# A gated attention kernel: the down-projection computed transposed, its result turned by transposing DMA copies

## Chip, cores, metric

The kernel runs on one core of one Trainium2 chip. The metric is the device time of one execution in microseconds (us), the median of several runs; lower is better.

## What is computed

S = 2048 tokens with D = 640 features, 32 heads of 20, a GLU with F = 1728 hidden features. All inputs and the output are bf16.

```python
xn  = layernorm(x)                         # (2048, 640)
q, k, v = split(xn @ wqkv)                 # 32 heads of 20
s   = softmax(q k^T / sqrt(20)) v  @ wo    # attention, then output projection
h   = sigmoid(xn @ w_gate) * (xn @ w_up)   # (2048, 1728)
g   = silu(h @ w_down)                     # the down-projection, then the gate
out = x + s * g
```

The softmax of 2048 x 2048 scores for 32 heads is most of the work.

## The kernel before

**Stages.** A first stage normalizes x, transposes it into `xnT` (features on partitions, four chunks of QC = 512 tokens) and computes the first keys, values and queries. The main stage works through NBLK = 32 blocks, each a group of GH = 4 heads times a chunk of 512 queries. A block has 64 score jobs (4 heads x 16 key tiles of 128): a matmul of TensorE (L889) into a PSUM bank, an exponential of the 128x512 scores, and a matmul with the values into `oacc` (L926). Most jobs have their exponential on ScalarE (`pt`, two jobs in one instruction, or `px`, one job; L82). The others go to VectorE, which builds the exponential from the bits of an integer: it converts the scores to int16 (`iv`, L1325) and makes three passes over four jobs at a time (`pb`, L1019, L1022, L1025). A short tail at the end does the last block and the last chunk's output.

**Order.** The order of instructions on TensorE, ScalarE, VectorE and GpSimd is written out at build time by a planner: a loop over simulated time in steps of 0.02 us that gives each engine its next instruction by fixed costs (`T_F`, `T_MM`, `T_IV` ...). Beside the score jobs it has a list of items: projections (`mk_k`, `mk_q`, `mk_v` ...), the GLU (`mk_gu`, `mk_down`) and the output (`mk_out`). An item is a chain of steps, such as matmuls on TensorE into one of three flexible PSUM banks, `bk`, then ScalarE, then VectorE; the planner puts it in between where TensorE has room. The same banks take score jobs for VectorE and for `px`. `LEAD` limits by how many us of work the GLU may run ahead of its due time. `M_ORD`, `DORD` and `XORD` choose the order in which banks are tried for an item, a VectorE job and a `px` job. On the chip each engine runs its list strictly in order and waits on semaphores.

**Transfers.** All but two of the main stage's transfers are issued by SP, one queue in order; an SP instruction whose data or buffer is not ready holds up everything behind it. The list `timed` holds transfers that the planner issues at a later simulated time. Per block there are: the softmax sums to DRAM and back (`ld`, L961; `lt`, L963), their reciprocals out and broadcast back (`rt`, L969; `rd`, L971; `rl`, L974), the normalized block into `oU` (L1009), and the next queries (`q`, L644, L645).

**The down-projection.** For each chunk of 512 tokens, after the 14 tiles of the hidden features `hT` are done, `mk_down` makes 8 items (4 token tiles `t4` x 2 halves `h` of the 640 features). Each multiplies a 128-token slice of `hT` (as weights) with 320 columns of `wd` in 14 steps; `cols` issues each step as four matmuls, one for each group of 32 output partitions. Then ScalarE takes a tanh (`td`, 128x320), and VectorE forms (tanh + 1) * ps, four times the silu, with tokens on partitions. For chunks 0 to 2 the product goes in fp32 into one of three buffers `gqs` (L740) and is stored to `gq_dram` (L742); `load_out` brings it back for the output stage (L771), where VectorE multiplies it with the projected attention (`otmp`, L795) and GpSimd adds x (L800). For chunk 3 it stays in SBUF, in two tiles `gql` (L736), and the tail reads it (L1096, L1102). `flush("o")` issues the additions that wait for GpSimd. SBUF tiles with a tag and `bufs=n` rotate through n buffers; a new one waits until the old contents have been read.

Of the kernel before, what the change touches and what calls it, by code (L numbers as in the profile page):

```python
# [27 lines left out]
UH = 6  # L28
UC = UH * DH

URGENT, ROUNDS, HOLD, SLACK, LEAD, LAG, D_LAST, D_LAST_END = 0.2, 6, 0.0, 0.0, 40.0, 2.0, 20, 20
M_ORD, WAIT3, FALL, M_END = 1, 0.2, 1, 2.0
NPT, NPX, NPB, NIV = 12, 5, 3, 3
XMAX, DQ, DORD, XORD, STARVE = 2, 1.4, 2, 0, 0.3

FILL_AT = 40
LOG2E = 1.4426950408889634
# [14 lines left out]
def kernel(  # L52
# [38 lines left out]
    persist = ctx.enter_context(tc.tile_pool(name="persist", bufs=1))  # L91
    wk = ctx.enter_context(tc.tile_pool(name="wk", bufs=2))

    gq_dram = dram.tile([S, D], FP32, name="gq_dram", tag="gqd", bufs=1)
    NU = (HEADS - PG * GH) // UH
    kD = [dram.tile([UC, S], BF16, name=f"kD{u}", tag=f"kD{u}", bufs=1) for u in range(NU)]
    qD = [dram.tile([UC, S], BF16, name=f"qD{u}", tag=f"qD{u}", bufs=1) for u in range(NU)]
# [346 lines left out]
    EL, PL = 0.15, 0.21  # L444
    T_F, T_PV, T_MM, T_MODE = 0.2133, 0.2133, 0.2133, 0.107
    T_IV, T_ON = 0.605, 0.60
    LATE, T_LT, T_OU, T_L2, T_RL = 1.0, 9.0, 1.5, 4.5, 5.6
    T_PASS = (0.1333, 0.1333, 0.27)

    def t_exp(n):  # L450
# [20 lines left out]
    def cols(out, lhsT, rhs, start, stop):  # L471
        for j in range(0, P, 32):
            nc.tensor.matmul(out[j:j + 32, :], lhsT=lhsT[:, j:j + 32], rhs=rhs, start=start, stop=stop,  # L473
                             tile_position=(0, j), skip_group_check=True)
# [189 lines left out]
    def mk_gu(c, kf, at):  # L664
        st = {}
        fs = fsz[kf]
        k2, ko = divmod(kf, 2)

        def alloc0():
            if (c, k2) not in wgu_tiles:  # L670
                load_wgu(c, k2)
            st["g"] = misc_ps()

        def alloc1():
            st["u"] = misc_ps()
            if ko == 0:
                n = c * NK2 + k2 + 1
                if n < NQC * NK2:
                    load_wgu(*divmod(n, NK2))

        def mm(key, i, kd):
            w = wgu_tiles[(c, k2)]
            cols(st[key], w[:, i, kd, ko * P:ko * P + P], xnT[:, c, kd, :], kd == 0, kd == KD - 1)

        def th():
            st["t"] = w2.tile([P, QC], BF16, tag="tnh", bufs=2, name="tnh")
            act_imm(st["t"][0:fs, :], st["g"][0:fs, :], ACT.Tanh, 0.5)

        def ev():
            return nc.vector.scalar_tensor_tensor(out=hT[0:fs, kf, :], in0=st["t"][0:fs, :], scalar=1.0,  # L690
                                                  in1=st["u"][0:fs, :], op0=ALU.add, op1=ALU.mult)

        def mm2(kd):
            cols(st["g"], wgu_tiles[(c, k2)][:, 0, kd, P:2 * P], xnT[:, c, kd, :], kd == 0, kd == KD - 1)

        def th2():
            st["t"] = w2.tile([P, QC], BF16, tag="tnh", bufs=2, name="tnh")
            act_imm(st["t"][fs:P, :], st["g"][0:fs, :], ACT.Tanh, 0.5)

        def ev2():  # L700
            return nc.vector.scalar_tensor_tensor(out=hT[0:fs, kf, :], in0=st["t"][fs:P, :], scalar=1.0,
                                                  in1=st["g"][fs:P, :], op0=ALU.add, op1=ALU.mult)
        if fs < P:
            return [Item([("PE", alloc0, [(T_MM, lambda kd=kd: mm2(kd)) for kd in range(KD)]),
                          ("ACT", 0.48, th2), ("DVE", 0.60, ev2, "free", mark("h", c, kf))], at)]
        return [Item([("PE", alloc0, [(T_MM, lambda kd=kd: mm("g", 0, kd)) for kd in range(KD)]),
                      ("ACT", 0.48, th, "free", mark("t", c, kf))], at),
                Item([("PE", alloc1, [(T_MM, lambda kd=kd: mm("u", 1, kd)) for kd in range(KD)]),
                      ("DVE", 0.60, ev, "free", mark("h", c, kf))], at, gates={1: [("t", c, kf)]})]

    gq_l = []

    def gq_last(t4):
        if len(gq_l) == t4 // 2:
            w = w2.tile([P, 2, KD, 2 * P], BF16, tag="wgu", bufs=2, name="gql")
            gq_l.append(w.rearrange("p i k f -> p (i k f)").bitcast(FP32))
        return gq_l[t4 // 2][:, t4 % 2 * D:(t4 % 2 + 1) * D]

    def mk_down(c, t4, h, at):
        st = {}  # L720
        tt = 4 * c + t4

        def alloc():
            st["ps"] = misc_ps()

        def mm(kf):
            cols(st["ps"][:, 0:HD], hT[:, kf, t4 * P:(t4 + 1) * P], wd[:, kf, h * HD:(h + 1) * HD],
                 kf == 0, kf == NFT - 1)

        def th():  # L730
            st["td"] = w2.tile([P, HD], BF16, tag="td", bufs=2, name="td")
            act_imm(st["td"], st["ps"][:, 0:HD], ACT.Tanh, 0.25)

        def ev():
            if c == NQC - 1:
                return nc.vector.scalar_tensor_tensor(out=gq_last(t4)[:, h * HD:(h + 1) * HD], in0=st["td"], scalar=1.0,  # L736
                                                      in1=st["ps"][:, 0:HD], op0=ALU.add, op1=ALU.mult)
            flush("o")
            gqs = w2.tile([P, HD], FP32, tag="gqs", bufs=3, name="gqs")
            ins = nc.vector.scalar_tensor_tensor(out=gqs, in0=st["td"], scalar=1.0, in1=st["ps"][:, 0:HD],  # L740
                                                 op0=ALU.add, op1=ALU.mult)
            nc.sync.dma_start(out=gq_dram[tt * P:(tt + 1) * P, h * HD:(h + 1) * HD], in_=gqs)  # L742
            return ins
        return Item([("PE", alloc, [(0.14, lambda kf=kf: mm(kf)) for kf in range(NFT)]),
                     ("ACT", 0.32, th), ("DVE", 0.40, ev, "free", mark("d", c, t4, h))], at, pre=[("h", c, kf) for kf in range(NFT)])


    FL, FG, FK = (NG - 1) * GC, (NG - 2) * GC, (KD - 1) * P
# [15 lines left out]
    def load_out(tt):  # L764
        if tt in out_tiles:
            return
        o2 = xfl[:, tt % 3 * KD * QC:tt % 3 * KD * QC + 3 * D]
        flush("o")
        out_tiles[tt] = (o2[:, 0:D], o2[:, D:3 * D].bitcast(FP32))
        nc.sync.dma_start(out=out_tiles[tt][0], in_=x2[tt * P:(tt + 1) * P, :])  # L770
        nc.sync.dma_start(out=out_tiles[tt][1], in_=gq_dram[tt * P:(tt + 1) * P, :])  # L771

    def mk_out(tt, h, at):
# [13 lines left out]
        def ev():  # L787
            xr, gqr = out_tiles[tt]
            sl = slice(h * HD, (h + 1) * HD)
            while sum(x[1] == "o" for x in pool_q) > 2:  # L790
                x = next(x for x in pool_q if x[1] == "o")
                pool_q.remove(x)
                x[2]()
            tmp = w2.tile([P, HD], FP32, tag="gqs", bufs=3, name="otmp")
            ins = nc.vector.scalar_tensor_tensor(out=tmp, in0=st["ps"][:, 0:HD], scalar=0.25,  # L795
                                                 in1=gqr[:, sl], op0=ALU.mult, op1=ALU.mult)

            def part(i):
                cs = slice(h * HD + i * HD // 2, h * HD + (i + 1) * HD // 2)
                add = nc.gpsimd.tensor_tensor(out=xr[:, cs], in0=tmp[:, i * HD // 2:(i + 1) * HD // 2], in1=xr[:, cs], op=ALU.add)  # L800
                if h == 1 and i == 1:
                    nc.sync.dma_start(out=out2[tt * P:(tt + 1) * P, :], in_=xr)
                return add
            for i in range(2):
                pool_q.append((now + 0.6, "o", lambda i=i: part(i)))
            return ins
        return Item([("PE", alloc, [(0.136, lambda kd=kd: mm(kd)) for kd in range(KD)]),
                     ("DVE", 0.40, ev, "free", mark("o", tt, h))], at, need=ALT + 1 + 2 * (tt // 4),
                    pre=[("d", tt // 4, t4, i) for t4 in range(4) for i in range(2)] + [("h", 2, kf) for kf in range(NFT)] + (
                        [("o", tt - 2, 1)] if h == 0 and tt > 1 else []))  # L810


# [1 line left out]
    for c in range(NQC):  # L814
        for kf in range(NFT):
            glu.append(lambda at, c=c, kf=kf: mk_gu(c, kf, at))
        for h in range(2):
            for t4 in range(4):
                glu.append(lambda at, c=c, t4=t4, h=h: [mk_down(c, t4, h, at)])
    for t in range(4 * NVP):  # L820
        v_at[(0, t)] = 0.0
    items = [mk_v(0, list(range(t, min(t + 3, TT))), 0.0) for t in range(4 * NVP, TT, 3)]
# [270 lines left out]
    xg = xl.rearrange("p (t u) -> p t u", u=D)  # L1093

    def t_main(t4):
        nc.vector.scalar_tensor_tensor(out=tmps[t4], in0=mains[t4], scalar=0.25, in1=gq_last(t4)[:, 0:512],  # L1096
                                       op0=ALU.mult, op1=ALU.mult)
        if t4 < 2:
            nc.gpsimd.tensor_tensor(out=tail[t4][:, 0:512], in0=tmps[t4], in1=tail[t4][:, 0:512], op=ALU.add)

    def t_rest(i):
        nc.vector.scalar_tensor_tensor(out=tmp[:, 2 * i:2 * i + 2, :],  # L1102
                                       in0=rest[i][:, 0:2 * EX].rearrange("p (t e) -> p t e", e=EX),
                                       scalar=0.25, in1=gq_l[i].rearrange("p (t u) -> p t u", u=D)[:, :, 512:D],
                                       op0=ALU.mult, op1=ALU.mult)
        (nc.vector if i else nc.gpsimd).tensor_tensor(out=xg[:, 2 * i:2 * i + 2, 512:D], in0=tmp[:, 2 * i:2 * i + 2, :],
                                                      in1=xg[:, 2 * i:2 * i + 2, 512:D], op=ALU.add)
# [420 lines left out]
```

## Time and profile before

| | |
|---|---|
| time, median of 3 runs | 803.18 us (802.27 to 803.32) |
| the profiled execution: its time, and its span from first to last instruction | 803.98 us, 802.3 us |
| granted TensorE clock | 1.000 |
| stores `gq_dram<-gqs` | 24 of 160 KB |
| loads `xnT<-gq_dram` | 12 of 320 KB |
| down-projection matmuls `bk<-wd,hT` | 1792, 128x320 |
| `td` on ScalarE, `gqs` and `gql` on VectorE | 32; 24 and 8, 128x320 |
| DMA queue q1, packets, data, share of 16 engines | 91447, 58.52 MB, 26.1% |

How to read the profile: PE is TensorE (PEld its weight loads), DVE VectorE, ACT ScalarE, POOL GpSimd, SP SyncE, whose DMA instructions stand as SPq. Rows of groups show line, engine, operation, output and inputs by the program's names with shape and type, a count, then busy time in us and mean duration of one in ns, then the idle time ahead of them and what ended it. Rows of the timeline start with the start time and the duration in us. Instructions of one engine overlap, so a duration is longer than the distance to the next start.

### The profile page before, as it was taken

To read this page: it belongs to the slowest core of one execution; us is meant where nothing else is said; L and a number is where in the kernel's file an instruction comes from. 1 tells how busy PE (TensorE), PEld (TensorE's weight loads), DVE (VectorE), ACT (ScalarE), POOL (GpSimd) and SP (SyncE) were. 2 spreads that over 40 slices of the span, in tenths; PEclk is the share of its full clock that TensorE was granted. 3 is DMA by queue.
4 is the path that set the end of the run, shared out by engine and by line. 5 is a ranking of instruction groups with operands and counts; after the bars stand their busy time and mean duration, and the time that the engine had idled before them with its cause. 6 is when DMAs were issued, how large, how long until landed. Compare 5 with 4: busy or idle time off the path is not lost.

```text
span 802.3 us, 25398 instructions
## 1 busy us (share of the span) xinstructions
PE 780.6 (97%) x10466; PEld 285.1 (36%) x10466; DVE 769.5 (96%) x1239; ACT 781.6 (97%) x991; POOL 106.2 (13%) x219
## 2 busy tenths in 40 slices
PE   8899999999999999999999999999999999999997
PEld 5523333333433323334332332333333233333333
DVE  7799999999999999989999999999999999999996
ACT  8799999999999999999999999999999999999994
POOL 7200000000000000000000010000000100502325
PEclk9999999999999999999999999999999999999999
DMA  5441212223122223222113133222311332330421
GB/s 162 133 130 49 69 40 75 63 66 81 47 63 66 73 72 100 52 57 71 49 47 94 53 86 76 76 79 58 98 37 61 91 89 53 106 103 23 141 62 62
DMA packets 91851, 60.47 MB, mean 75 GB/s; under 512 B 34891, under 2 KB 85627, under 8 KB 91735
## 3 DMA queue, kind: packets, MB, share of 16 engines
q1 hardware_dynamic: 91447, 58.52, 26.1%
q8 instruction: 82, 1.34, 0.7%
q14 instruction: 34, 0.28, 0.1%
q10 hardware_dynamic: 288, 0.33, 0.1%
HBM read 45.18 MB, written 11.09 MB: 70 GB/s over the span
## 4 chain that ended last, share of the span: by engine, by line
PE 48%; ACT 39%; DVE 6%; issue 5%; DMA 1%; SPq 0%; POOL 0%; DVEq 0%; ACTq 0%; POOLq 0%
ACT pt L82 31%; PE bk L473 20%; PE scA L889 15%; PE oacc L926 10%; ACT px L82 4%; ACT tnh L82 2%; DVE iv L1325 2%; DVE pb L1025 1%; PE bk L889 1%; ACT td L82 1%; PE tp L292 1%; DVE pb L1022 0%; DMA xt<-in_A_x_dram 0%; PE scrap L398 0%; PE psk L142 0%
## 5 line engine op out<-in xcount | busy, mean ns | idle before, releaser
L82 ACT ACTIVATE pt<-scA 128x1024 bf16<-128x1024 f32 (+1 forms) x709 | 708.8, 1189 | 1.0 <-PE scA L889 0.4
L1325 DVE TENSOR_SCALAR iv<-bk 128x512 int16<-128x512 f32 x500 | 332.9, 684 | 12.0 <-PE bk L889 9.6
L889 PE MATMUL scA<-q,kT 32*128 32x512 bf16 x1412 | 275.9, 382 | 8.7 <-ACT pt L82 3.3
L889 PE MATMUL bk<-q,kT 32*128 32x512 bf16 x636 | 207.4, 383 | 0.0
L889 PEld LDWEIGHTS <-kT 32*128 32x128 bf16 x2048 | 88.5, 91 | 262.0 <-issue 250.6
L926 PE MATMUL oacc<-pt,v 128*21 128x512 bf16 x1412 | 178.7, 381 | 0.7 <-ACT pt L82 0.7
L926 PE MATMUL oacc<-pb,v 128*21 128x512 bf16 x1000 | 161.4, 382 | 0.0
L473 PE MATMUL bk<-xnT,wgu 128*32 128x512 bf16 x2160 | 157.3, 383 | 0.5 <-DVE iv L1325 0.2
L1025 DVE TENSOR_TENSOR pb<-iv,pb 128x2048 bf16<-128x2048 bf16 x125 | 152.5, 1220 | 0.7
L979 POOL TENSOR_TENSOR on_bf<-on,rl 128x128 bf16<-128x128 f32 x116 | 54.4, 472 | 627.3 <-DVE iv L1325 170.4
L82 ACT ACTIVATE px<-bk 128x512 bf16<-128x512 f32 x136 | 101.4, 763 | 1.7 <-POOL hT L1167 1.6
L1019 DVE TENSOR_SCALAR pb<-iv 128x2048 int16<-128x2048 int16 x125 | 87.1, 697 | 0.4
L473 PE MATMUL bk<-wd,hT 128*32 128x320 bf16 x1792 | 87.0, 302 | 0.3 <-DVE iv L1325 0.2
L1022 DVE TENSOR_SCALAR pb<-iv 128x2048 int16<-128x2048 int16 x125 | 86.7, 693 | 0.0
L926 PEld LDWEIGHTS <-v 128*21 128x21 bf16 x2548 | 53.9, 91 | 76.0 <-issue 53.5
L473 PEld LDWEIGHTS <-wgu 128*32 128x32 bf16 x2160 | 44.4, 95 | 64.3 <-issue 45.9
L473 PEld LDWEIGHTS <-hT 128*32 128x32 bf16 x1792 | 37.5, 95 | 38.5 <-issue 32.9
L473 PE MATMUL bk<-xnT,wu 128*32 128x512 bf16 x640 | 48.5, 384 | 0.6 <-DVE iv L1325 0.2
L926 PE MATMUL oacc<-px,v 128*21 128x512 bf16 x136 | 46.7, 381 | 0.0
L82 ACT ACTIVATE tnh<-bk 128x512 bf16<-128x512 f32 (+1 forms) x56 | 43.4, 776 | 0.1
L690 DVE SCALAR_TENSOR_TENSOR hT<-tnh,bk 128x512 bf16<-128x512 bf16 x52 | 35.4, 681 | 1.0 <-PE bk L889 0.3
L800 POOL TENSOR_TENSOR xnT<-otmp,xnT 128x160 bf16<-128x160 f32 x48 | 28.2, 607 | 40.4 <-PE bk L889 15.9
(119 smaller groups left out, 413.6 us busy)
## 6 DMA issues: line engine op xcount, KB each, us to landing
rl<-rd SPq DMA_DIRECT2D x124, 64.0 KB
wgu<-in_B_w_gate_dram SPq DMA_DIRECT2D x24, 320.0 KB
wgu<-in_B_w_up_dram SPq DMA_DIRECT2D x24, 320.0 KB
gq_dram<-gqs SPq DMA_DIRECT2D x24, 160.0 KB
xnT<-gq_dram SPq DMA_DIRECT2D x12, 320.0 KB
xt<-in_A_x_dram SPq DMA_DIRECT2D x16, 160.0 KB
xnT<-in_A_x_dram SPq DMA_DIRECT2D x16, 160.0 KB
out_dram<-xnT SPq DMA_DIRECT2D x14, 160.0 KB
```

Of the source, the lines that this page charges most:

```text
L82: return nc.scalar.add_instruction(mybir.InstActivation(func=func, name=nc.get_next_instruction_name(), engine=ENG.Activation, ins=[nc.sca ...
L292: nc.tensor.transpose(out=tps[k][:, kd, :], in_=xns[k][:, kd * P:(kd + 1) * P], identity=ident)
L473: nc.tensor.matmul(out[j:j + 32, :], lhsT=lhsT[:, j:j + 32], rhs=rhs, start=start, stop=stop, tile_position=(0, j), skip_group_check=True)
L690: return nc.vector.scalar_tensor_tensor(out=hT[0:fs, kf, :], in0=st["t"][0:fs, :], scalar=1.0, in1=st["u"][0:fs, :], op0=ALU.add, op1=ALU. ...
L800: add = nc.gpsimd.tensor_tensor(out=xr[:, cs], in0=tmp[:, i * HD // 2:(i + 1) * HD // 2], in1=xr[:, cs], op=ALU.add)
L889: nc.tensor.matmul(dst, lhsT=kTs[gc_of(b)[0] % 2][32 * j:32 * j + 32, kt * P:(kt + 1) * P], rhs=qts[b % 3][32 * j:32 * j + 32, :], start=T ...
L926: nc.tensor.matmul(oacc[32 * j:32 * j + DH + 1, :], lhsT=lhsT, rhs=u["src"], start=first, stop=last, tile_position=(0, 32 * j), skip_group ...
L979: ins = nc.gpsimd.tensor_tensor(out=on_bf[:, cs], in0=on[:, cs], in1=rl[:, cs], op=ALU.mult)
L1019: ins = nc.vector.tensor_scalar(out=pb[:, 0, :, :].bitcast(I16), in0=iv, scalar1=0x7F80, scalar2=1, op0=ALU.bitwise_and, op1=ALU.bitwise_or)
L1022: ins = nc.vector.tensor_scalar(out=pb[:, 1, :, :].bitcast(I16), in0=iv, scalar1=0x007F, scalar2=0x3F00, op0=ALU.bitwise_and, op1=ALU.bitw ...
L1025: ins = nc.vector.tensor_tensor(out=pb[:, 1, :, :], in0=iv.bitcast(BF16), in1=pb[:, 1, :, :], op=ALU.mult)
L1325: beat(nc.vector.tensor_scalar(out=d["iv"][:, j, :], in0=bank[bk], scalar1=B_OFF, scalar2=0.0, op0=ALU.add, op1=ALU.max))
```

## The change

The down-projection is computed with features on partitions: 5 items per chunk, one for each 128 features `e`, with a slice of `wd` as weights and all 512 tokens of `hT` as the moving operand, in 14 steps. Tanh and product are 128x512. The product goes in bf16 into `gqs`, now with one buffer, and a DMA copy that transposes, from SBUF to SBUF, turns it to tokens on partitions: into `g4` (one buffer) for chunks 0 to 2, into `gql` for chunk 3. It is issued on SP 0.8 us (`T_GT`) after the simulated time of the product. For chunks 0 to 2 a store of `g4` to `gq_dram`, now bf16, follows 5.8 us (`T_GO`) after the product. The output stage and the tail read bf16. The planner's costs of the item follow (`T_MM` for a step, 0.48 and 0.60 us for tanh and product), `tnh` gets a third buffer and takes the tanh of the down-projection too, `otmp` has a tag of its own, and four of the planner's settings change.

```diff
-URGENT, ROUNDS, HOLD, SLACK, LEAD, LAG, D_LAST, D_LAST_END = 0.2, 6, 0.0, 0.0, 40.0, 2.0, 20, 20
-M_ORD, WAIT3, FALL, M_END = 1, 0.2, 1, 2.0
+URGENT, ROUNDS, HOLD, SLACK, LEAD, LAG, D_LAST, D_LAST_END = 0.2, 6, 0.0, 0.0, 30.0, 2.0, 20, 20
+M_ORD, WAIT3, FALL, M_END = 0, 0.2, 1, 2.0
-XMAX, DQ, DORD, XORD, STARVE = 2, 1.4, 2, 0, 0.3
+XMAX, DQ, DORD, XORD, STARVE = 2, 1.4, 0, 1, 0.3
-    gq_dram = dram.tile([S, D], FP32, name="gq_dram", tag="gqd", bufs=1)
+    gq_dram = dram.tile([S, D], BF16, name="gq_dram", tag="gqd", bufs=1)
-    LATE, T_LT, T_OU, T_L2, T_RL = 1.0, 9.0, 1.5, 4.5, 5.6
+    LATE, T_LT, T_OU, T_L2, T_RL, T_GT, T_GO = 1.0, 9.0, 1.5, 4.5, 5.6, 0.8, 5.8
...
-    def mk_down(c, t4, h, at):
+    def mk_down(c, e, at):
         def mm(kf):
-            cols(st["ps"][:, 0:HD], hT[:, kf, t4 * P:(t4 + 1) * P], wd[:, kf, h * HD:(h + 1) * HD],
-                 kf == 0, kf == NFT - 1)
+            cols(st["ps"], wd[:, kf, e * P:(e + 1) * P], hT[:, kf, :], kf == 0, kf == NFT - 1)
         def th():
-            st["td"] = w2.tile([P, HD], BF16, tag="td", bufs=2, name="td")
-            act_imm(st["td"], st["ps"][:, 0:HD], ACT.Tanh, 0.25)
+            st["td"] = w2.tile([P, QC], BF16, tag="tnh", bufs=3, name="td")
+            act_imm(st["td"], st["ps"], ACT.Tanh, 0.25)
         def ev():
-            if c == NQC - 1:
-                return nc.vector.scalar_tensor_tensor(out=gq_last(t4)[:, h * HD:(h + 1) * HD], in0=st["td"], scalar=1.0,
-                                                      in1=st["ps"][:, 0:HD], op0=ALU.add, op1=ALU.mult)
-            flush("o")
-            gqs = w2.tile([P, HD], FP32, tag="gqs", bufs=3, name="gqs")
-            ins = nc.vector.scalar_tensor_tensor(out=gqs, in0=st["td"], scalar=1.0, in1=st["ps"][:, 0:HD],
+            gqs = w2.tile([P, QC], BF16, tag="gqs", bufs=1, name="gqs")
+            ins = nc.vector.scalar_tensor_tensor(out=gqs, in0=st["td"], scalar=1.0, in1=st["ps"],
                                                  op0=ALU.add, op1=ALU.mult)
-            nc.sync.dma_start(out=gq_dram[tt * P:(tt + 1) * P, h * HD:(h + 1) * HD], in_=gqs)
+            es = slice(e * P, (e + 1) * P)
+            g4 = w2.tile([P, 4, P], BF16, tag="g4", bufs=1, name="g4") if c < NQC - 1 else gq_last()[:, :, es]
+            timed.append((now + T_GT, lambda: nc.sync.dma_start_transpose(out=g4, in_=gqs)))
+            if c < NQC - 1:
+                timed.append((now + T_GO, lambda: nc.sync.dma_start(
+                    out=gq_dram[c * QC:(c + 1) * QC, es].rearrange("(t p) u -> p t u", p=P), in_=g4)))
             return ins
-        return Item([("PE", alloc, [(0.14, lambda kf=kf: mm(kf)) for kf in range(NFT)]),
-                     ("ACT", 0.32, th), ("DVE", 0.40, ev, "free", mark("d", c, t4, h))], at, pre=[("h", c, kf) for kf in range(NFT)])
+        return Item([("PE", alloc, [(T_MM, lambda kf=kf: mm(kf)) for kf in range(NFT)]),
+                     ("ACT", 0.48, th), ("DVE", 0.60, ev, "free", mark("d", c, e))], at, pre=[("h", c, kf) for kf in range(NFT)])
...
-            tmp = w2.tile([P, HD], FP32, tag="gqs", bufs=3, name="otmp")
+            tmp = w2.tile([P, HD], BF16, tag="ot", bufs=3, name="otmp")
```

Left out: the loops and names that follow from it (5 items instead of 8 per chunk, one `gql` tile in bf16 instead of two in fp32, `tnh` with three buffers, half the bytes in `load_out`).

More of the change, by code (lines that the diff above doesn't have):

```diff
@@ L685, in th @@
         def th():
-            st["t"] = w2.tile([P, QC], BF16, tag="tnh", bufs=2, name="tnh")
+            st["t"] = w2.tile([P, QC], BF16, tag="tnh", bufs=3, name="tnh")
             act_imm(st["t"][0:fs, :], st["g"][0:fs, :], ACT.Tanh, 0.5)
@@ L696, in th2 @@
         def th2():
-            st["t"] = w2.tile([P, QC], BF16, tag="tnh", bufs=2, name="tnh")
+            st["t"] = w2.tile([P, QC], BF16, tag="tnh", bufs=3, name="tnh")
             act_imm(st["t"][fs:P, :], st["g"][0:fs, :], ACT.Tanh, 0.5)
@@ L711, with gq_last @@
     gq_l = []
-    def gq_last(t4):
-        if len(gq_l) == t4 // 2:
+    def gq_last():
+        if not gq_l:
             w = w2.tile([P, 2, KD, 2 * P], BF16, tag="wgu", bufs=2, name="gql")
-            gq_l.append(w.rearrange("p i k f -> p (i k f)").bitcast(FP32))
-        return gq_l[t4 // 2][:, t4 % 2 * D:(t4 % 2 + 1) * D]
-    def mk_down(c, t4, h, at):
+            gq_l.append(w.rearrange("p i k f -> p (i k f)")[:, 0:4 * D].rearrange("p (t u) -> p t u", u=D))
+        return gq_l[0]
+    def mk_down(c, e, at):
         st = {}
-        tt = 4 * c + t4
         def alloc():
@@ L766, in load_out @@
             return
-        o2 = xfl[:, tt % 3 * KD * QC:tt % 3 * KD * QC + 3 * D]
+        o2 = xfl[:, tt % 3 * KD * QC:tt % 3 * KD * QC + 2 * D]
         flush("o")
-        out_tiles[tt] = (o2[:, 0:D], o2[:, D:3 * D].bitcast(FP32))
+        out_tiles[tt] = (o2[:, 0:D], o2[:, D:2 * D])
         nc.sync.dma_start(out=out_tiles[tt][0], in_=x2[tt * P:(tt + 1) * P, :])
@@ L808, in mk_out @@
                      ("DVE", 0.40, ev, "free", mark("o", tt, h))], at, need=ALT + 1 + 2 * (tt // 4),
-                    pre=[("d", tt // 4, t4, i) for t4 in range(4) for i in range(2)] + [("h", 2, kf) for kf in range(NFT)] + (
+                    pre=[("d", tt // 4, i) for i in range(KD)] + [("h", 2, kf) for kf in range(NFT)] + (
                         [("o", tt - 2, 1)] if h == 0 and tt > 1 else []))
@@ L816 @@
             glu.append(lambda at, c=c, kf=kf: mk_gu(c, kf, at))
-        for h in range(2):
-            for t4 in range(4):
-                glu.append(lambda at, c=c, t4=t4, h=h: [mk_down(c, t4, h, at)])
+        for e in range(KD):
+            glu.append(lambda at, c=c, e=e: [mk_down(c, e, at)])
     for t in range(4 * NVP):
@@ L1095, in t_main @@
     def t_main(t4):
-        nc.vector.scalar_tensor_tensor(out=tmps[t4], in0=mains[t4], scalar=0.25, in1=gq_last(t4)[:, 0:512],
+        nc.vector.scalar_tensor_tensor(out=tmps[t4], in0=mains[t4], scalar=0.25, in1=gq_last()[:, t4, 0:512],
                                        op0=ALU.mult, op1=ALU.mult)
@@ L1103, in t_rest @@
                                        in0=rest[i][:, 0:2 * EX].rearrange("p (t e) -> p t e", e=EX),
-                                       scalar=0.25, in1=gq_l[i].rearrange("p (t u) -> p t u", u=D)[:, :, 512:D],
+                                       scalar=0.25, in1=gq_last()[:, 2 * i:2 * i + 2, 512:D],
                                        op0=ALU.mult, op1=ALU.mult)
```

## The prediction

> **What bounds the kernel now.** I read the page first: part 1 for the load of each engine, part 4 for the chain that ended last. The first line is the span; the second gives busy time, share of the span and instructions; the third the shares of the chain.
>
> ```profile
> span 802.3 us, 25398 instructions
> PE 780.6 (97%) x10466; PEld 285.1 (36%) x10466; DVE 769.5 (96%) x1239; ACT 781.6 (97%) x991; POOL 106.2 (13%) x219
> ...
> PE 48%; ACT 39%; DVE 6%; issue 5%; DMA 1%; SPq 0%; POOL 0%; DVEq 0%; ACTq 0%; POOLq 0%
> ```
>
> Three engines are at 96 to 97%, and the chain passes from PE to ACT and back. No single engine is the bound: what is saved on one counts only in the part of the chain that it carries, while what stops one of them soon stops the others, since all run in an order fixed in advance. DMA is 1% of the chain; the 16 DMA engines have room. Next, the stretches in which the down-projection runs (its 8 items of a chunk lie at 362 to 418 us and 564 to 614 us for chunks 1 and 2), as busy time by stage:
>
> ```profile
> 362.00:418.00 56.00, 54.78 (x824) 21.80 (x820) 55.55 (x88) 55.94 (x72) 5.22 (x12) 1.00 0.19 57
> 564.00:614.00 50.00, 49.08 (x775) 19.32 (x775) 49.24 (x79) 49.84 (x63) 3.65 (x8) 1.00 0.23 71
> ```
>
> After the length come PE, PEld, DVE, ACT and POOL, then granted clock, DMA share, GB/s. DVE is busy 55.55 of 56 us: a wait put before one of its instructions finds no idle time to hide in. The chain cut to 560 to 620 us says who carries the end there:
>
> ```profile
> by line: ACT pt L82 33.5%; PE bk L473 23.1%; PE scA L889 19.6%; PE oacc L926 10.8%; issue 6.7%; ACT td L82 4.2%; ACT tnh L82 1.0%; PE bk L889 0.9%; ACT px L82 0.8%; ACTq L82 0.2%
> ```
>
> PE has 54% of it (23.1 + 19.6 + 10.8 + 0.9), ACT 40%, DVE none: DVE is full but just in time.
>
> **The work removed and added.** Engine instructions overlap, so I price one by the distance from its start to the next start in the timeline (start, duration, engine):
>
> ```profile
> 303.01 1.26 PE L473 MATMUL bk<-xnT,wgu 128*32 128x512 bf16 x20
> ...
> 372.05 0.48 ACT L82 ACTIVATE td<-bk 128x320 bf16<-128x320 f32 x1
> 372.37 2.92 ACT L82 ACTIVATE pt<-scA 128x1024 bf16<-128x1024 f32 x3
> 375.08 0.70 ACT L82 ACTIVATE px<-bk 128x512 bf16<-128x512 f32 x1
> 375.55 2.06 ACT L82 ACTIVATE pt<-scA 128x1024 bf16<-128x1024 f32 x2
> ...
> 387.06 1.00 PE L473 MATMUL bk<-wd,hT 128*32 128x320 bf16 x24
> ...
> 396.45 0.68 DVE L959 COPY on<-oacc 128x512 f32<-128x512 f32 x1
> 397.05 0.68 DVE L1022 TENSOR_SCALAR pb<-iv 128x2048 int16<-128x2048 int16 x1
> 397.65 0.48 DVE L740 SCALAR_TENSOR_TENSOR gqs<-td,bk 128x320 f32<-128x320 bf16 x1
> 398.05 0.68 DVE L1325 TENSOR_SCALAR iv<-bk 128x512 int16<-128x512 f32 x1
> ```
>
> PE: matmuls go in groups of four, side by side. The x24 row is six groups: less the last one's 0.302 us (mean of this group on the page), (1.00 - 0.302)/5 = 0.140 us for a 320-wide group. The x20 row gives (1.26 - 0.383)/4 = 0.219 us for a 512-wide one. Before: 1792/4 = 448 groups x 0.140 = 62.7 us. After: 4 chunks x 5 items x 14 = 280 groups x 0.219 = 61.3 us. Saved 1.4 us.
> ACT: a 320-wide tanh takes 372.37 - 372.05 = 0.32 us, a 512-wide activation 375.55 - 375.08 = 0.47 us. 32 x 0.32 - 20 x 0.47 = 0.8 us saved.
> DVE: 398.05 - 397.65 = 0.40 us against 397.05 - 396.45 = 0.60 us for 512 columns out of PSUM. 32 x 0.40 - 20 x 0.60 = 0.8 us saved. Out and final stages keep shape and PSUM operand, so bf16 in them I count at nothing; if a bf16 product with PSUM were quicker, DVE would win less than the 0.4 us of one such instruction in all, off the chain.
> On the path: 1.4 x 0.54 + 0.8 x 0.40 = 1.1 us. Bounds: none of it, if ACT and DVE hold each other up, to 1.4 + 0.8 = 2.2 us.
>
> **The transfers.** 24 stores of 160 KB go, with the three buffers of gqs and the forced release of GpSimd's adds ahead of each (`flush("o")`). In come 20 transposing copies of 128x512 in bf16 (128 KB), issued by SP, and 15 stores of 128 KB; the 12 loads of L771 halve. In bandwidth that is nothing: DMA is at 0.19 to 0.23 in those windows. What counts is the order of waits: gqs and g4 have one buffer each. The copy waits on SP for g4, that is for the store before; the store waits on SP for the copy; and the next DVE product waits for gqs, that is for the copy before. Queued behind that product on DVE are the conversions (L1325) that empty the PSUM banks, on which PE waits for its next scores, and ACT for PE. Queued behind the copy and the store on SP are the loads of q and rl and the copies into oU.
>
> The trace of before has no transposing copy. From below, a plain copy between two SP instructions of which the second reads what the first wrote:
>
> ```profile
> 372.90 0.54 SPq L961 DMA_DIRECT2D ld<-on  x1
> ...
> 374.62 0.33 SPq L963 DMA_DIRECT2D lt<-ld  x1
> ```
>
> 1.7 us from issue to use. From above: queue q1 moved 91447 packets in 26.1% of 16 engines over 802.3 us, 0.037 us of an engine for a packet. 128 KB in pieces of 256 bytes (one row of a 128x128 block) are 512 pieces, 32 an engine, 1.2 us; in pieces of 32 bytes they are 4096, 256 an engine, 9.4 us. With about 1.5 us of latency the bounds are 1.7 and 11 us. I take 5 us: it lies between the ends, and is what the changed order itself leaves between copy and store (5.8 - 0.8).
>
> The Trainium skill (VectorE: DVE Perf Modes, The three transpose paths) gives 1309 ns for a 128x128 bf16 block through the DMA crossbar; four in a row would be an estimate of 5.2 us. Against it, the Trainium skill (Advanced Engine Details and Errata, X-Bar Transpose (TRN2)) says that such copies are as fast as regular ones, which would put it at the lower end. No run so far shows which.
>
> Spacing of the items: the gqs products of chunk 1 start at 385.2, 391.2, 397.6, 403.5, 410.2 and 415.6 us, 6.1 us apart on average, for 14 x 0.140 = 2.0 us of PE work each. A wide item has 14 x 0.219 = 3.1 us, so it comes every 9.4 us; the closest pair of before (4.0 us, 585.0 to 589.0) becomes 6.2 us. The loop of gqs: 0.8 us to the issue, 0 to 3 us in SP's queue (its runs of oU and q copies take 2 to 3.6 us), 5 us for the copy: 6 to 9 us. The loop of g4: copy 5, store about 2.2: 7 to 8 us. Both are near the spacing. I take 6 of the 20 products to wait 1.0 us: 6 us of DVE, of which PE's share of the chain (0.54) follows: 3.3 us lost. Bounds: zero (copies at 1.7 us), and 20 x 1.5 x 0.54 = 16 us (copies at 7 us or more, each product late).
>
> **The order.** LEAD, M_ORD, DORD and XORD change which bank serves whom and how early the GLU runs. Nothing in the trace prices that; the nearest row is the idle time before DVE's conversions:
>
> ```profile
> L1325 DVE TENSOR_SCALAR iv<-bk 128x512 int16<-128x512 f32 x500 | 332.9, 684 | 12.0 <-PE bk L889 9.6
> ```
>
> Half of the 12.0 us more or less, times 0.54, is 3.2 us either way. I take zero: no reason for a sign. At the end gql is needed at 794 us and its last product starts at 770.9 us, so 23 us cover the last copy; without that cover the copy's 5 us would add in full.
>
> **Sum.** The profiled execution: 803.98 us, of which 802.3 us is the span and 1.7 us lies around it. 803.98 - 1.1 + 3.3 + 0 = 806.2 us, 2.2 us more. The median of the runs is 803.18, so the forecast is 805.4 us.
>
> **Rivals.**
> 1. The copies stay hidden (other side). At 2 to 3 us a copy, the loops close in 5 to 6 us, under any spacing; then the saving counts and nothing is lost, with PE as the engine that decides: 803.18 - 2.2 = 801.0 us at its bound. It decides wherever a copy lands within 5 us of the product. For it: 75 GB/s of mean traffic, and PE's 54%. Chance 0.25.
> 2. The new order decides: 3.2 us less with the 1.1 saved is 798.9 us; 3.2 us more on top of the forecast is 808.6 us. Chance 0.12 for less, 0.08 for more.
> 3. Gain and waits cancel, 801.6 to 804.8 us, about 803. Chance 0.18.
> 4. The copies are of the slow kind (7 us and more): 803.2 + 15 = 818 us. For it, 32-byte pieces; against it, the 5 us allowed. Chance 0.06.
> The forecast itself has 0.31.
>
> A change within 0.2% (1.6 us) is about what a measurement of this kernel can tell from none. Faster: 0.25 + 0.12, less 0.02 of rival 1 that falls within the bound: 0.35. Same: 0.18 + 0.02 = 0.20. Slower: 0.31 + 0.08 + 0.06 = 0.45. Two signs share the chance: the forecast alone would be 804.8 to 808 us. The range runs from rival 2's lower end, 799.0 us, to 811.0 us, about half of the upper bound of the waits; it leaves out rival 4 and the outer parts of the others.
>
> **What would show it.** Right: DVE idle time before the new product, released by a DMA; SP waits of some us at the copy and the store; PE groups at 0.219 us. Wrong: no DMA releaser on DVE and copies of 2 us (rival 1); a change of the idle time of L1325 and of ACT's pt far from the down stretches (rival 2). A copy that SP itself is busy issuing for us would shift the loss to the loads behind it.

## Result: slower by 0.65%, and the profile after

The changed kernel takes 808.57 us (median of 6 runs, 807.13 to 809.11) against 803.15 us for the kernel before (6 runs): a ratio of 1.0065, 95% interval 1.0054 to 1.0075, or 5.4 us more. The profiled execution is the second fastest of the six, 807.15 us with a span of 805.4 us; it shows 3.1 us of the loss in its span.

The page of the changed kernel, span and busy time (from the down-projection on, line numbers are 1 or 2 lower than in the kernel before, that of `gqs` 6 lower):

```profile
span 805.4 us, 24045 instructions
PE 775.0 (96%) x9794; PEld 263.0 (33%) x9794; DVE 769.4 (96%) x1227; ACT 781.6 (97%) x983; POOL 106.4 (13%) x219
```

PE's busy time fell by 5.6 us and the span grew. The stages show where. Busy time by stage, of the changed kernel:

```profile
362.00:418.00 56.00, 54.42 (x710) 17.71 (x704) 55.33 (x85) 55.86 (x72) 5.17 (x11) 1.00 0.25 59
690.00:750.00 60.00, 55.74 (x788) 18.71 (x787) 56.57 (x89) 57.94 (x71) 15.89 (x31) 1.00 0.25 66
750.00:790.00 40.00, 36.24 (x515) 12.27 (x507) 36.11 (x58) 36.61 (x44) 20.02 (x32) 1.00 0.30 91
```

and of the kernel before, the last two:

```profile
690.00:750.00 60.00, 58.95 (x911) 22.09 (x912) 58.58 (x95) 59.52 (x73) 19.51 (x35) 1.00 0.31 94
750.00:790.00 40.00, 39.31 (x614) 15.17 (x606) 38.94 (x61) 39.63 (x50) 15.36 (x23) 1.00 0.28 82
```

In the down-projection of chunk 1 (362 to 418 us) all engines are as full as before: DVE 55.33 of 56 us. From 690 us on, ACT loses 1.6 us of 60 and then 3.0 us of 40, and PE and DVE lose with it. The copies of `oacc` into `on` mark the blocks: the one of block 28 starts at 723.6 us (before: 723.3), that of block 29 at 748.5 (747.4), that of block 30 at 771.0 (770.3), and the one of block 31, in the tail, at 794.7 (791.0). So 0.3 us of the loss had arisen by 723 us; the rest comes in the last 80 us, 2.9 us of it behind 771 us. Three of the waits that grew most, summed over the run (engine and line, what it waited for, us, times, longest):

```profile
DVE rt L967 <- DMA lt<-ld: 4.3, 2, 2.8
ACT pt L82 <- PE bk L887: 3.4, 4, 2.1
PE bk L473 <- DVE iv L1323: 2.9, 4, 2.3
```

Before, they stood at 1.7, 0.2 and 0.7 us. They belong together, as the timeline around 732 us shows (in brackets the idle time ahead and what ended it):

```profile
731.88 0.25 DVE L967 RECIPROCAL rt<-lt 128x16 f32<-128x16 f32 x1 [2.75 <-DMA lt<-ld]
...
733.86 0.68 DVE L1323 TENSOR_SCALAR iv<-bk 128x512 int16<-128x512 f32 x1
...
734.60 1.26 PE L473 MATMUL bk<-hT,wd 128*32 128x512 bf16 x20 [2.25 <-DVE iv L1323]
...
736.28 3.77 ACT L82 ACTIVATE pt<-scA 128x1024 bf16<-128x1024 f32 x4 [2.06 <-PE bk L887]
```

DVE stands 2.75 us at the reciprocal of block 28's softmax sums. Behind it in DVE's order is the conversion that empties a PSUM bank; PE waits 2.25 us for that bank, and ACT 2.06 us for the scores that PE then makes. The wait passes through all three engines nearly whole. Its cause is on SP:

```profile
724.88 0.76 SPq L1007 DMA_DIRECT2D oU<-on_bf  x1
725.75 1.24 SPq L738 DMA_TRANSPOSE gql<-gqs  x1
727.04 0.75 SPq L1007 DMA_DIRECT2D oU<-on_bf  x1
727.90 0.53 SPq L959 DMA_DIRECT2D ld<-on  x1
728.48 1.51 SPq L1007 DMA_DIRECT2D oU<-on_bf  x2
730.09 0.42 SPq L961 DMA_DIRECT2D lt<-ld  x1
```

The sums are ready at 723.6 + 0.7 us, but `ld` is issued at 727.9 and `lt` at 730.1, behind copies into `oU` of the block before and one transposing copy. The first of these copies was itself held 3.8 us for GpSimd's `on_bf` (before: 3.6 us). The planner put the reciprocal T_L2 = 4.5 us after the `on` copy; up to block 27 it leaves T_LT = 9.0 us. The reciprocal came 8.3 us after the start of the `on` copy here, 6.7 us before. The wait itself is in the kernel before too, shorter:

```profile
730.05 0.25 DVE L969 RECIPROCAL rt<-lt 128x16 f32<-128x16 f32 x1 [1.28 <-DMA lt<-ld]
```

It has 0.4 us more in block 29 and none in block 30, where the changed kernel waits again, in the stretch that loses most:

```profile
778.00 0.25 DVE L967 RECIPROCAL rt<-lt 128x16 f32<-128x16 f32 x1 [1.60 <-DMA lt<-ld]
```

In all the waits for `lt` grew by 2.6 us, beside the 3.1 us of the span.

The new transfers do what was asked of them. SP around the second chunk's first copy:

```profile
373.40 1.26 SPq L738 DMA_TRANSPOSE g<-gqs  x1
374.76 0.52 SPq L136 DMA_DIRECT2D wv<-in_A_wqkv_dram  x1
375.94 0.36 SPq L740 DMA_DIRECT2D gq_dram<-g  x1
```

The store waits for the copy and starts 2.54 us after it. SP itself is occupied 1.2 us by a transposing copy (median; 2.1 us at most), against 0.3 to 0.5 us by most plain ones (0.7 us by one into `oU`). The new product on DVE has these idle times ahead of it in all its 20 instances:

```profile
L734 DVE SCALAR_TENSOR_TENSOR gqs<-td,bk x20: 677/680/689, 205.5 to 744.2; 128x512 bf16<-128x512 bf16 x20
...
  ACT td L82: 0.6, 2
```

None is ended by a DMA: `gqs` with one buffer never held DVE up.

### The profile page after: what moved, and what is told of

Its sections match the earlier page's. It is cut to its first block, busy times and chain, and to the rows that moved or that the text cites. A ratio compares the mean times of both kernels' runs of the same rounds, so it can differ in the third digit from the quotient of the medians.

```text
span 805.4 us, 24045 instructions
## 1 busy us (share of the span) xinstructions
PE 775.0 (96%) x9794; PEld 263.0 (33%) x9794; DVE 769.4 (96%) x1227; ACT 781.6 (97%) x983; POOL 106.4 (13%) x219
## 5 line engine op out<-in xcount | busy, mean ns | idle before, releaser
L82 ACT ACTIVATE pt<-scA 128x1024 bf16<-128x1024 f32 x707 | 698.8, 1165 | 3.8 <-PE bk L887 3.4
L1323 DVE TENSOR_SCALAR iv<-bk 128x512 int16<-128x512 f32 x500 | 332.3, 683 | 10.6 <-PE bk L887 8.6
L887 PE MATMUL bk<-q,kT 32*128 32x512 bf16 x642 | 204.0, 383 | 1.7 <-DVE otmp L794 1.0
L924 PE MATMUL oacc<-pt,v 128*21 128x512 bf16 x1406 | 185.3, 382 | 0.9 <-ACT pt L82 0.8
L887 PEld LDWEIGHTS <-kT 32*128 32x128 bf16 x2048 | 85.5, 91 | 288.1 <-issue 278.2
L473 PE MATMUL bk<-xnT,wgu 128*32 128x512 bf16 x2160 | 159.2, 383 | 0.8
L473 PE MATMUL bk<-hT,wd 128*32 128x512 bf16 x1120 | 82.6, 383 | 2.8 <-DVE iv L1323 2.4
L924 PE MATMUL oacc<-px,v 128*21 128x512 bf16 x142 | 48.6, 382 | 0.0
L82 ACT ACTIVATE tnh<-bk 128x512 bf16<-128x512 f32 (+1 forms) x56 | 41.7, 745 | 0.1
L799 POOL TENSOR_TENSOR xnT<-otmp,xnT 128x160 bf16<-128x160 bf16 x48 | 28.2, 607 | 45.8 <-DVE pb L1020 26.4
L473 PEld LDWEIGHTS <-wd 128*32 128x32 bf16 x1120 | 20.7, 95 | 35.6 <-issue 29.3
```

Source lines behind the costliest of these rows:

```text
L82: return nc.scalar.add_instruction(mybir.InstActivation(func=func, name=nc.get_next_instruction_name(), engine=ENG.Activation, ins=[nc.sca ...
L887: nc.tensor.matmul(dst, lhsT=kTs[gc_of(b)[0] % 2][32 * j:32 * j + 32, kt * P:(kt + 1) * P], rhs=qts[b % 3][32 * j:32 * j + 32, :], start=T ...
L924: nc.tensor.matmul(oacc[32 * j:32 * j + DH + 1, :], lhsT=lhsT, rhs=u["src"], start=first, stop=last, tile_position=(0, 32 * j), skip_group ...
L1323: beat(nc.vector.tensor_scalar(out=d["iv"][:, j, :], in0=bank[bk], scalar1=B_OFF, scalar2=0.0, op0=ALU.add, op1=ALU.max))
```

## Experiments

Ratios are against runs of the kernel before on the same chip, in brackets the 95% interval. The edits are given in short. Three theories: **copies** (the transposing copies and their single buffers, my forecast), **order** (the four planner settings), **form** (wide items are harder to place).

**The old settings under the changed kernel.**
```diff
-LEAD 30.0, M_ORD 0, DORD 0, XORD 1
+LEAD 40.0, M_ORD 1, DORD 2, XORD 0
```


> The changed kernel with the four planner settings of before (LEAD 40, M_ORD 1, DORD 2, XORD 0); items, copies and bf16 stay changed. Theory 'order' (the four settings cost the 5.4 us): at or below 803 us, and the ACT time lost between 690 and 790 us is back. Theory 'copies' (the transposing copies on SP cost it): 807 to 809 us, as changed. Theory 'form' (wide items are harder to place, whatever the settings): 806 us or more.


803.41 us, ratio 1.000 (0.9989 to 1.0011). The transposed form, its 20 copies and bf16 stay, and the whole loss is gone. 'Copies' and 'form' fall as causes by themselves.

**The new settings under the kernel before.**
```diff
-LEAD 40.0, M_ORD 1, DORD 2, XORD 0
+LEAD 30.0, M_ORD 0, DORD 0, XORD 1
```


> The kernel before with the four new planner settings (LEAD 30, M_ORD 0, DORD 0, XORD 1) and nothing else. 'Order': about 808 us, the whole loss without any copy. 'Copies' and 'form': within 2 us of 803 us.


810.56 us, ratio 1.0084 (1.0071 to 1.0097). The settings alone cost 6.6 us, without one transposing copy. DVE's wait for `lt` is 5.5 us in this profile, 3.6 us of it at once, in block 29, and 1.4 us in block 27.

**No copies.**
```diff
-g4 = ... bufs=1; dma_start_transpose(out=g4, in_=gqs)
+g4 = ... bufs=2; the product is written straight into g4 or gql
```


> The changed kernel without its 20 transposing copies: DVE writes its product straight into g4 (two buffers) or gql, and the store follows as before; the turn of each block is left out, and the order on PE, ACT, DVE and GpSimd is that of the changed kernel. 'Copies': back to 803 us or below, and the 2.75 us DVE wait for the softmax sums near 731 us is gone. 'Order' and 'form': 807 to 809 us; the one wait is worth at most 2 us of it.


806.75 us, ratio 1.0036 (1.0022 to 1.0049): between the two, and the wait near 731 us is smaller, not gone. `ld` is issued at 727.5 and `lt` at 729.3 us, only 0.4 and 0.8 us earlier than with the copies.

```profile
731.02 0.25 DVE L965 RECIPROCAL rt<-lt 128x16 f32<-128x16 f32 x1 [1.64 <-DMA lt<-ld]
```

Up to block 28 every `on` copy starts within 0.5 us of the changed kernel's, so the copies of chunks 0 to 2 cost nothing that shows. The difference, 2.3 us (0.0029 of the time), arises after that, with 1.1 us less of this wait.

**More time for the sums in the last blocks.** This put the wait itself to the test.
```diff
-T_L2 = 4.5
+T_L2 = 7.0
```


> The changed kernel with T_L2 = 7.0 instead of 4.5: in the last blocks the planner puts the reciprocal of the softmax sums 2.5 us later into DVE's order. If DVE's wait of 2.75 us for lt (block 28, behind copies in SP's queue) stands on the path: 805.5 to 807 us. If not, or if the later reciprocal delays the last blocks by as much: 808 us or more.


804.31 us, ratio 1.0008 (0.9999 to 1.0016): more came back than I had expected. `lt` is issued as late as before the edit (730.1 us), but DVE now has three other instructions ahead of the reciprocal and its wait for `lt` falls to 0.5 us in all:

```profile
728.95 0.68 DVE L1020 TENSOR_SCALAR pb<-iv 128x2048 int16<-128x2048 int16 x1
729.67 1.23 DVE L1023 TENSOR_TENSOR pb<-iv,pb 128x2048 bf16<-128x2048 bf16 x1
730.82 0.68 DVE L1323 TENSOR_SCALAR iv<-bk 128x512 int16<-128x512 f32 x1
731.83 0.25 DVE L967 RECIPROCAL rt<-lt 128x16 f32<-128x16 f32 x1 [0.33 <-DMA lt<-ld]
```

A new theory, **late sums**, against **order in general**: what the settings cost is that DVE waits for `lt` in blocks 28 to 30. The edit of T_L2 changes the order of the last blocks too, so the wait was next taken away under an order that stays.

**The wait taken away, order kept.**
```diff
-beat(nc.vector.reciprocal(out=rt, in_=lt), False)
+beat(nc.vector.reciprocal(out=rt, in_=lts[-2] if b >= NBLK - 4 else lt), False)
```
`lts` is the list of the `lt` tiles so far, so `lts[-2]` holds the sums of the block before.


> The changed kernel, every order the same, but in the last blocks (28 to 30) the reciprocal reads the softmax sums of the block before, which have long landed (so these blocks are scaled by other sums). Theory 'late sums' (DVE's wait for lt in the last blocks, 4.3 us in the profile, carries the loss): the wait is gone and the time falls by 3 to 5 us, to 804 to 806 us. Theory 'order in general' (the new bank order places work worse in the last 80 us, the wait only sits in it): 807.5 us or more.


804.04 us, ratio 1.0012 (1.0003 to 1.0021). By the ratios that is 0.0053 less than the changed kernel's, 4.3 us, with no other instruction moved. Its profile, of an execution of 806.48 us, shows no wait of DVE for `lt`:

```profile
728.74 1.28 DVE L1326 TENSOR_SCALAR iv<-bk 128x512 int16<-128x512 f32 x2
729.94 0.24 DVE L970 RECIPROCAL rt<-lt 128x16 f32<-128x16 f32 x1
```

Yet its span is only 0.6 us shorter than the changed kernel's. From block 28's `on` copy to block 29's it takes 22.7 us (changed kernel: 24.9), and from block 30's to the tail's 22.7 us (23.7). In between, where neither waits for `lt`, it takes 24.2 us (22.5). There the granted TensorE clock, third from the right, was lower; first this run, then the changed kernel:

```profile
748.00:771.00 23.00, 21.07 (x280) 6.55 (x279) 19.39 (x33) 20.04 (x25) 9.20 (x16) 0.87 0.34 99
748.00:771.00 23.00, 20.32 (x293) 6.89 (x296) 20.77 (x35) 21.75 (x26) 9.73 (x17) 1.00 0.33 99
```

The run's eleven executions part by this clock, taken as a mean over the span: the six with 0.996 or 0.997 took 803.1 to 804.0 us, 803.7 us on average, like the kernel before on this chip; the five with 0.992 to 0.995 took 805.6 to 806.5 us. So with the wait gone no loss is left in the first six, and what the ratio still shows goes with the clock. No run tests the clock by itself. The profiles of the changed kernel and of the kernel before hold 1.00 from 24 to 790 us; with the new settings on the kernel before it fell too, to 0.72 from 760 to 770 us, so not all of those 6.6 us need be the wait.

**The same on the kernel before, with the new and with its own settings.** T_L2 = 7.0 in both.


> The kernel before with the four new settings and T_L2 = 7.0. 'Late sums': the 6.6 us that the settings cost are mostly back, 803.5 to 806 us. 'Order in general': 808 us or more.


807.70 us, ratio 1.0054 (1.0042 to 1.0066). A miss: only 2.4 of 6.6 us came back. Its profile is of an execution of 810.57 us, where the other five took 807.2 to 807.9 us. It still waits 4.6 us for `lt`. Block 29's wait falls from 3.6 to 1.9 us, but its `lt` is issued 7.3 us after the `on` copy, so 7.0 us are not enough there. The other 2.7 us are in block 27, to which T_L2 does not apply.

> The kernel before with T_L2 = 7.0 alone. It waits 1.7 us for lt in all: 'late sums' gives at most 1.7 us less, 802.3 to 804 us; 'order in general' gives no direction, within 2 us of before.


803.13 us, ratio 0.9994 (0.9986 to 1.0003). No difference that shows. Its profile waits 1.3 us.

**Old settings and T_L2 = 7.0 under the changed kernel**, the candidate to beat both.


> The changed kernel with the four old settings and T_L2 = 7.0, the candidate to beat both: it waits 2.1 us for lt without it. 'Late sums': 801.5 to 803 us, up to 2 us below before. 'Order in general': within 2 us of before, either way.


803.20 us, ratio 0.9994 (0.9985 to 1.0003). DVE never waits for `lt`. It is 0.7% faster than the changed kernel and not to be told from the kernel before: no version that was run beats both.

**No copies and T_L2 = 7.0**, to price the copies once the wait is gone.


> The changed kernel with T_L2 = 7.0 and without its transposing copies (the turn of each block left out; the order on PE, ACT, DVE and GpSimd is that of the T_L2 kernel). 'Late sums': with the wait for lt gone the copies cost nothing more, so the same as with T_L2 alone, 803.5 to 805.5 us. Theory 'copies cost by themselves' (gqs or g4 with one buffer, SP's queue): 1.5 us or more below it, 801 to 803 us.


806.29 us, ratio 1.0026 (1.0016 to 1.0036): slower than with copies and T_L2 = 7.0 (1.0008). Neither expectation held. Without the copies SP's queue runs otherwise, and in this profile block 29's `lt` comes 7.0 us after its `on` copy: DVE waits 2.4 us there. So the copies have no price of their own that these runs can show. Seven of its eight executions had a granted clock of 0.988 to 0.995, so part of the time may be the clock's.

**The last chunk's copies later.**
```diff
-timed.append((now + T_GT, ... dma_start_transpose ...))
+timed.append((now + (T_GT if c < NQC - 1 else 7.5), ...))
```


> The changed kernel with the copies of the last chunk issued 7.5 us after the product instead of 0.8, so that they fall behind the sums' transfers in SP's queue; all else the same, and nothing is left out. If the copy ahead of ld is what makes block 28's sums late: that wait shrinks from 2.75 to about 1.5 us and the time is that without copies, 806 to 807 us. If SP's copies into oU make them late and the transposing copy doesn't matter: 808 to 809 us.


808.18 us, ratio 1.0045 (1.0031 to 1.0059). The test did not separate what it was made for: the copy moved past `ld` but still fell ahead of `lt`, and block 28's wait stayed at 2.8 us.

```profile
727.99 0.53 SPq L959 DMA_DIRECT2D ld<-on  x1
728.56 0.74 SPq L1007 DMA_DIRECT2D oU<-on_bf  x1
729.34 1.24 SPq L738 DMA_TRANSPOSE gql<-gqs  x1
730.69 0.52 SPq L961 DMA_DIRECT2D lt<-ld  x1
```

**Which of the settings.** LEAD alone back to 40, and the three bank orders alone back.


> The changed kernel with LEAD = 40 as before, the three new bank orders kept. If running the GLU less far ahead costs the time: 803 to 804.5 us. If the bank orders do: 807 to 810 us. 'Late sums' says that the time follows DVE's wait for lt in blocks 28 to 30, whichever setting moves it: about 1 us of time for 1 us of wait.


807.98 us, ratio 1.0046 (1.0033 to 1.0058); the wait for `lt` is 4.4 us.

> The changed kernel with the three bank orders of before, LEAD = 30 kept. The other half of the pair: 803 to 804.5 us if the bank orders cost the time, 807 to 810 us if LEAD does; by 'late sums' again as its wait for lt.


804.39 us, ratio 1.0003 (0.9993 to 1.0013); the wait is 2.3 us, once. The bank orders carry the loss; LEAD at most a small part.

**All kernels side by side**, by DVE's wait for `lt` in the profile:

| kernel | wait for lt, us | ratio |
|---|---|---|
| changed, old settings, T_L2 7.0 | none | 0.9994 |
| changed, sums of the block before | none | 1.0012 |
| changed, T_L2 7.0 | 0.5 | 1.0008 |
| before, T_L2 7.0 | 1.3 | 0.9994 |
| before | 1.7 | 1 |
| changed, old settings | 2.1 | 1.0000 |
| changed, old bank orders | 2.3 | 1.0003 |
| changed, no copies, T_L2 7.0 | 2.4 | 1.0026 |
| changed, no copies | 3.4 | 1.0036 |
| changed | 4.3 | 1.0065 |
| changed, LEAD 40 | 4.4 | 1.0046 |
| changed, last copies later | 4.4 | 1.0045 |
| before, new settings, T_L2 7.0 | 4.6 | 1.0054 |
| before, new settings | 5.5 | 1.0084 |

A straight line through them has a slope of 1.1 us of time for 1 us of wait, with a correlation of 0.89. The wait comes from one execution each, in three rows the longest of its run (sums of the block before; last copies later; before, new settings, T_L2 7.0), and the ratio from several, so the rows need not fall in order; up to 2.3 us of wait, the ratio stays within 0.0012 of 1. That the wait carries most of the loss of the changed kernel, 4.3 of 5.4 us, is shown by the run that removes it under the same order; for the other kernels the table speaks for it and no more.

## Why the prediction was right and where it was not

**Direction and size.** Slower was forecast at 805.4 us within 799 to 811; measured 808.57. The loss over before, 5.4 us, is more than double the 2.2 us of the sum, and the mechanism of the forecast was wrong: the waits that were to cost the time did not occur, and the step put at zero carried it. That the sign and the range held is luck.

**The work saved (1.1 us).** The terms held as prices: an x20 row of the wide matmuls lasts 1.26 us in the changed kernel too, 0.219 us for a group, and the counts are those of the diff. As a gain on the path it is not seen: with equal settings the ratio is 1.000, give or take 0.9 us. The lower bound, none of it, was nearer, in stretches where ACT is busy 55.86 of 56 us.

**The copy (5 us).** It takes about 2.5 us from its issue to the store that waits for it. The rows gave 1.7 to 11 us, and I took the middle because the order left 5 us between copy and store; that allowance was room, not a measurement. The rule of the Trainium skill of 1309 ns for a 128x128 block (VectorE: DVE Perf Modes, The three transpose paths), four in a row an estimate of 5.2 us, is twice too long here. The other rule of the Trainium skill (Advanced Engine Details and Errata, X-Bar Transpose (TRN2)), as fast as a regular DMA, is near: 2.5 us for 128 KB beside 1.7 us for 8 KB, though SP is held 1.2 us to issue it.

**The waits on gqs and g4 (3.3 us).** This step failed: no product waited. The products of chunk 1 came 7.5 to 11.0 us apart, the closest of all 7.3 us, close to the 6.2 to 9.4 us of the forecast; with 2.5 us a copy the loops close well within that, which is what rival 1 said. The 6.1 us from which the spacing was scaled came from the last six of that chunk's eight products; all eight, from 366.4 to 415.6 us, are 7.0 us apart, so even the forecast's own rows gave more room.

**The order (0, with 3.2 us either way).** Here the loss arose. I had no reason for a sign, and priced it by the idle time of DVE's conversions; that fell from 12.0 to 10.6 us. The row that carried it was in the waits of before, `rt` on `lt` with 1.7 us: an allowance of 4.5 us already overrun in two of the last three blocks. I named the loads of q and rl and the copies into `oU` as what is queued behind the new instructions on SP, and left out `ld` and `lt`, for which DVE waits. Rival 2 had the right cause and its upper number, 808.6 us. That number holds 3.3 us of copy waits that did not occur, so its fit is luck. Of its signs, the idle time ahead of ACT's `pt` did grow, from 1.0 to 3.8 us, but that of the conversions fell: the order cost time by where the sums fall in SP's queue.

**What stays open.** Of the loss, 4.3 us follow DVE's wait; about 1 us (0.0012 of the time, interval 0.0003 to 0.0021) is left over. It is found only in the executions with a granted clock of 0.995 or less; why the clock falls in some executions, and whether the order has a part in it, is not shown. The clock is not the only spread: with the old bank orders the times run from 802.8 to 806.8 us at 0.996 to 0.999. How a bank order shifts the copies into `oU` ahead of `ld` was not followed through the planner.

## What to carry to other kernels

In an order written out by hand, look for the allowances that the trace already overruns, however small the wait: a queue in order can turn a new transfer, or another order, into more of it, and engines that are full pass most of it on (2.06 of 2.75 us here). When a change comes with new settings, run the settings alone and the change alone before arguing about the mechanism. And price a new transfer by what its reader and its queue do; its bandwidth said nothing here. Before reading one execution's span against another's, compare the clock that each was granted.

## What the runs showed of the hardware

The store that waits for a transposing copy of 128x512 bf16 from SBUF to SBUF started 2.5 us after the copy's issue, but the copy occupied SP for 1.2 us, against 0.3 to 0.7 us for the plain ones. A wait of 2.75 us on DVE came out at ACT as 2.06 us; the buffers between these engines, each about 96% busy, took up the other 0.7 us, an estimate from this one wait. And the same order of instructions took 24.2 us from block 29's `on` copy to block 30's at a granted clock of 0.87, and 22.5 us at 1.00.
